# Decay masks of a linear-attention start written by blocks of the triangle, without filling products, with its steps reordered

## The chip, the cores and the metric

The kernel runs on one core of a Trainium2 chip. The metric is the device time of one execution in microseconds (us); the kernel before takes 508.67 us (median of three runs, 508.61 to 508.83). The engines are named as in the profile: PE is TensorE, PEld its weight loads, DVE is VectorE, ACT is ScalarE, POOL is GpSimd, SP is SyncE. PSUM is the memory that PE writes its products to; it is used here in banks of 128 x 512 float32, 2 in the pool `pacc`, 4 in `pmm` and 2 in `patt`.

## The reference

Three layers follow one another: a chunked linear attention with decays (4 batches, 8 heads, 768 steps, head width 32, state 16), a gated feed-forward layer with an RMS norm (256 to 1536 to 256), and a second feed-forward layer with a time shift (256 to 1024 to 256).

```python
for c in range(nc):
    cum = np.cumsum(la, axis=-1)                       # la: log of the decays a
    L = np.exp(cum[:, :, :, None] - cum[:, :, None, :])
    L = L * causal                                     # 0 where j > i
    M = np.einsum('bhin,bhjn->bhij', Cc, Bc) * L
    y_intra = np.einsum('bhij,bhjd->bhid', M, xc)
    y_inter = np.einsum('bhin,bhnd->bhid', Cc, state) * decay_to_i[:, :, :, None]
    ...
xn = x / rms * rms_g
x = (silu(xn @ w_gate) * (xn @ w_val)) @ w_out
...
k = np.maximum(xk @ w_k, 0.0); v = k * k @ w_v
out = sigmoid(xr @ w_r) * v
```

## The kernel before

The kernel works in chunks of 128 steps, six in all (t = 0 to 5), with all four batches side by side: a tile has 128 partitions and 512 columns. While PE multiplies chunk t through the first feed-forward layer (`ffn1`, twelve units u of 128 hidden columns; `g` and `v` are the two products of a unit, `hf` their gated product, `h` its split into two float32r parts, `x` the sum over units), the other engines prepare the attention of the next chunk. Every product with a weight is made of three float32r products (lines 748, 749, 750: high by high, low by high, high by low). The weights arrive as float64, and DVE and ACT convert them while the first chunk runs (`wst`, `wt`, and at last `wgh` and `wgl`, `wvh` and `wvl`, `woh` and `wol`; lines 268, 275, 273, 279, 288, 289).

Before the first product of `ffn1` the attention of chunk 0 has to be done in full, and that of chunk 1 is begun. Their decays L are made on PE and ACT: a bank `Eb` holds, for 4 heads, the matrix (j on partitions, i on columns) of cum(i) - cum(j). First it gets a mask, 0 where i >= j and -30000 elsewhere: a bf16 product of the unit matrix `eye` with `before`, repeated for 4 heads (`spread_eye`, line 380). Then a product with 32 rows adds the sums (`spread_e`, line 393; two batches lie on different rows of the array and their products start together), and ACT takes the exponential (`exp_e`, tile `E`). Chunks 0 and 1 take 8 banks each, all from the four of `pmm`.

The string `START` is the order in which the steps of this beginning are written down: `q` is `spread_eye` ahead of time, `e` and `x` the decays of chunks 0 and 1, `s` and `S` the score products `sc`, `m` and `M` the masking on DVE, `y` the products with x, `n` the RMS norm, `c`, `P` and `z` weight conversions, `k` constants. `fill` puts in extra float32 products (line 637) that nobody reads; `FILL` says where, once in each half of the norm `n`. The written order is not the order of the program: `arrange` runs a list scheduler (`Order`) over all instructions with prices of its own (and with those of `costs`), and fixes the order on each engine. In it an earlier written step wins where two are ready. So a change at the start moves instructions much later as well.

In `ffn1` the tiles g and v take their banks from `pmm` in turn, so that v of unit 3 gets its bank when `hf` of unit 1 (DVE, line 792) has read v of unit 1. The attention of chunk 1 puts its products `y<-Ch,Sf` (line 569), `y<-E,x` (line 527) and `y<-x,Bd` (line 533) between those of the first units.

Of the kernel before, what the change touches and what calls it, by code (L numbers as in the profile page):

```python
# [9 lines left out]
F32 = mybir.dt.float32  # L10
# [6 lines left out]
P = 128  # L17
# [4 lines left out]
T = NB * P  # L22
# [14 lines left out]
        (99, 99, 99, 99, 99, 99, 99, 99, 99, 99, 99, 99, 99))  # L37

HIGH_ACT = ((0, 1, 2, 3, 4, 5, 6, 7, 10, 11), (2, 7))
START = 's0 k0 q0 q1 l0 p0 e0 l1 p1 m0 m1 e2 s1 m2 m3 y0 y1 y2 n0 c0 c1 P0 y3 x0 x2 d0 L0 u0 L1 n1 P1 z0 t0 S0 M1 k1 M0'  # L40
SPARE, LATE_E, BEHIND = ((0, 0), (0, 1), (1, 0)), (), (('n0', 'n1'),)
LOW_POOL, ON_POOL = (), ()

SUB_DVE, MIX_UNIT = tuple(range(27)), 9
MEANS, SPREAD, LOAD_E = (6, 10), 11, (3, 6)
WARM, COLD, HALVED, FILL = (9,), 11, 2, {('n', 0): 1, ('n', 2): 1}

TABLES = {AF.Ln: "natural_log_exp_and_others", AF.Exp: "natural_log_exp_and_others",
          AF.Silu: "silu_and_others", AF.Sigmoid: "sigmoid_and_others"}
# [28 lines left out]
def tile_kernel(ctx: ExitStack, tc, a_c, x_t, B_t, B_s, C_s, B_p, C_p, C_h, kc,  # L78
                w_gate, w_val, w_out, w_k, w_v, w_r, out):
    nc = tc.nc  # L80
    slots, chains, groups, gates, urgent, ranks, costs = {}, [], [], [], [], {}, {}
# [15 lines left out]
    pacc = Pool("pacc", 2, bass.MemoryType.PSUM)  # L97
    pmm = Pool("pmm", 4, bass.MemoryType.PSUM)
# [50 lines left out]
    eye = wp.tile([P, P], BF16, name="eye")  # L149
    before = wp.tile([P, P], BF16, name="before")  # L150
# [154 lines left out]
    A = {c: {} for c in range(NC + 2)}  # L305
# [68 lines left out]
            placed(left, spread_l[c], ML, 2)  # L374

    def spread_eye(c, b):
        for half in range(2):
            pool, tag = (pacc, "acc") if c and b in LATE_E else (pmm, "mm")
            ps = A[c]["Eb", b, half] = pool.tile([P, T], F32, tag=tag, name="Eb")
            mm = nc.tensor.matmul(ps, eye, before.unsqueeze(1).broadcast_to([P, 4, P]), start=True, stop=False)  # L380
            if len(costs) < COLD:
                costs[mm.ins.name] = 427.0
            A[c]["eye", b, half] = mm.ins.name

    def spread_e(c, pair):
        for b in pair:
            if ("Eb", b, 0) not in A[c]:
                spread_eye(c, b)
        for half in range(2):
            for b in pair:  # L390
                g = slice(32 * b, 32 * b + 32)
                eyes = [A[c]["eye", k, half] for k in pair]
                mm = nc.tensor.matmul(A[c]["Eb", b, half], spread_l[c][g, half], spread_r[c][g].rearrange("p h i -> p (h i)"),
                                      start=False, stop=True)
                chains.extend((one, mm.ins.name) for one in eyes)
                if b % 2:
                    costs[mm.ins.name] = 90.0
# [354 lines left out]
    def ffn1(t, hook):  # L752
        xn = [A[t]["xn", k] for k in range(2)]
        acc, hs = [], {}

        def contract(u):
            h = hs.pop(u)
            if u == 0:
                acc.extend(pacc.tile([P, T], F32, tag="acc", name=f"x2_{m}") for m in range(2))
            for m in range(2):  # L760
                mm3(acc[m], wo, u, m, h, u == 0, u == NU - 1)

        gv = {}

        def up(u, parts=(slice(0, T),)):
            for s in parts:
                for n, w in (("g", wg), ("v", wv)):
                    if (n, u) not in gv:
                        gv[n, u] = pmm.tile([P, T], F32, tag="mm", name=n)
                    for k in range(2):  # L770
                        mm3(gv[n, u], w, k, u, xn[k], k == 0, k == 1, s)

        for u in range(NU):
            hook("ab", u)
            if t == 0 and u < HALVED:
                if u == 0:
                    for s in cols:
                        for w in range(HALVED):
                            up(w, (s,))
            else:  # L780
                up(u)
            g, v = gv.pop(("g", u)), gv.pop(("v", u))
            if t <= 1:
                sl = t2("sl")
            elif u % 2 == 0:
                sls = t4("sl")
                sl = sls[:, 0, :]
            else:
                sl = sls[:, 1, :]
            hf = t2("hf")  # L790
            tabled(out=sl, in_=g, func=AF.Silu)
            nc.vector.tensor_mul(hf, sl, v)  # L792
            hs[u] = pair("hl", "h")
            split(hs[u], hf, act_e,
                  pool_e if t == 1 and u in LOW_POOL else vec_e)
            if u >= 2:
                contract(u - 2)

        def tail():
            for u in (NU - 2, NU - 1):  # L800
                contract(u)

        return acc, tail
# [89 lines left out]
    def warm_up(n, pool, tag):  # L893
        w = pool.tile([P, T], F32, tag=tag, name="warm")
        for k in range(n):
            mm = nc.tensor.matmul(w, ones, ones.unsqueeze(1).broadcast_to([P, 4, P]), start=True, stop=True)
            if len(costs) < COLD:
                costs[mm.ins.name] = 427.0 if costs else 900.0
# [26 lines left out]
    def exps(c, b):  # L925
        spread_e(c, (b, b + 1))
        for k in (b, b + 1):
            for half in range(2):
                exp_e(c, k, half)
# [29 lines left out]
    def late_decayed(_):  # L959
        for b in range(NB):  # L960
            decayed_b(0, b)

    stage = dict(e=lambda b: exps(0, b), s=lambda two: scores(0, two), S=lambda two: scores(1, two), M=lambda b: masked(1, b), L=lambda part: load_x(1, part), z=more, t=lambda _: table(AF.Silu), m=masks, y=squares, n=norms, c=convert0, P=lambda u: first[3](u),
                 l=sums, p=placed_e, x=lambda b: exps(1, b), d=late_decayed, u=lambda _: states0(),
                 k=lambda n: (norm_eye, scan_masks)[n](), w=lambda n: warm_up(n, patt, "at"), q=lambda b: spread_eye(0, b))
    for step in START.split():
        at = len(list(nc.cur_bb.bb.instructions))
# [27 lines left out]
    for t in range(NC):  # L995
        c, e = t + 1, t + 2
# [105 lines left out]
        x2, tail = ffn1(t, hook)  # L1102
        if t == 0:
# [9 lines left out]
            x2 = [x2s[:, m] for m in range(2)]  # L1113
# [298 lines left out]
```

## Time and profile before

| | before |
|---|---|
| median of three runs | 508.67 us (508.61 to 508.83) |
| profiled execution | 508.6 us, of it the span 506.6 us |
| PE busy | 500.2 us, 99% of the span |
| DVE busy | 375.7 us, 74% |
| ACT busy | 307.9 us, 61% |
| first product of `ffn1` starts | 24.88 us |
| granted TensorE clock in the records | 1.00 |

The span runs from the first to the last instruction; the profiled execution has 2.0 us around it. A timeline row gives a start, the length of the group, the engine, the line, the operation, the tiles and the number of instructions; plain float32 products (`sc`, `y`, `ss`, the filling ones) have two records each. A product's record lasts longer than the distance to the next one, because products overlap; the distance between two starts is what it costs.

### The profile page before, as it was taken

What the parts mean: (1) busy time and instruction counts of PE and PEld (TensorE: products, weight loads), DVE (VectorE), ACT (ScalarE), POOL (GpSimd) and SP (SyncE); (2) the same over time, 40 slices, a digit from 0 to 9 for tenths busy, and PEclk for the clock granted to TensorE, in tenths of its full rate; (3) what the DMA queues carried; (4) which work ended last, traced back from release to release, by engine and by line L of the source; (5) the groups of instructions that cost most, each with busy time, mean ns of one, the idle gap of its engine ahead of it and who ended that gap; (6) DMA issues with size and microseconds to landing.
All of it is one profiled execution on the core that took longest, in us unless ns stands there. A gap on an engine that the chain in (4) does not pass through costs nothing.

```text
span 506.6 us, 7497 instructions
## 1 busy us (share of the span) xinstructions
PE 500.2 (99%) x2869; PEld 406.8 (80%) x2869; DVE 375.7 (74%) x610; ACT 307.9 (61%) x509; POOL 10.4 (2%) x26
## 2 busy tenths in 40 slices
PE   8999999999999999999999999999999999999997
PEld 4687887788888888888888888888888888888885
DVE  6899998988698965479995659996628763335672
ACT  5999798566589744457763456764358643345552
POOL 1100000000010000010000010000000000000000
PEclk9999999999999999999999999999999999999999
DMA  8868755342321220152111141110000000000101
GB/s 257 230 204 276 261 175 193 105 137 93 123 85 43 78 82 13 57 174 77 42 58 68 46 162 44 65 48 36 0 1 1 18 25 1 1 1 0 42 0 42
DMA packets 23283, 42.60 MB, mean 84 GB/s; under 512 B 3136, under 2 KB 6720, under 8 KB 23248
## 3 DMA queue, kind: packets, MB, share of 16 engines
q1 hardware_dynamic: 20496, 33.41, 20.0%
q10 hardware_dynamic: 2752, 8.72, 5.1%
q8 instruction: 22, 0.36, 0.3%
q14 instruction: 13, 0.11, 0.1%
HBM read 38.52 MB, written 3.34 MB: 83 GB/s over the span
## 4 chain that ended last, share of the span: by engine, by line
PE 91%; DVE 5%; ACT 2%; issue 1%; DMA 1%; DVEq 0%; ACTq 0%
PE v L748 10%; PE v L750 10%; PE v L749 10%; PE g L748 6%; PE x L748 6%; PE x L749 6%; PE x L750 6%; PE g L749 6%; PE g L750 6%; PE kp L748 4%; PE kp L750 4%; PE kp L749 4%; PE y L527 2%; PE sc L442 1%; PE rps L750 1%; PE rps L749 1%
## 5 line engine op out<-in xcount | busy, mean ns | idle before, releaser
L792 DVE TENSOR_TENSOR hf<-sl,v 128x512 f32<-128x512 f32 x72 | 49.0, 683 | 50.0 <-PE v L750 49.5
L140 ACT CAST h<-hf 128x512 fp32r<-128x512 f32 x72 | 44.4, 617 | 60.8 <-DVE hf L792 60.7
L133 ACT ACTIVATE sl<-g 128x512 f32<-128x512 f32 x72 | 42.8, 595 | 44.9 <-PE g L750 44.6
L143 DVE TENSOR_TENSOR h<-hf,h 128x512 fp32r<-128x512 f32 x72 | 50.5, 701 | 24.1 <-ACT h L140 24.1
L748 PE MATMUL g<-xn,wgh 128*128 128x512 f32 (+1 forms) x148 | 58.0, 392 | 0.4 <-DVE E L514 0.4
L749 PE MATMUL g<-xn,wgl 128*128 128x512 f32 (+1 forms) x148 | 57.0, 385 | 0.4 <-DVE wgl L289 0.4
L748 PE MATMUL v<-xn,wvh 128*128 128x512 f32 (+1 forms) x148 | 57.0, 385 | 0.0
L750 PE MATMUL g<-xn,wgh 128*128 128x512 f32 (+1 forms) x148 | 56.8, 384 | 0.0
L749 PE MATMUL v<-xn,wvl 128*128 128x512 f32 (+1 forms) x148 | 56.8, 384 | 0.0
L750 PE MATMUL v<-xn,wvh 128*128 128x512 f32 (+1 forms) x148 | 56.8, 383 | 0.0
L749 PE MATMUL x<-h,wol 128*128 128x512 f32 x144 | 56.3, 391 | 0.0
L748 PE MATMUL x<-h,woh 128*128 128x512 f32 x144 | 55.8, 391 | 0.1
L750 PE MATMUL x<-h,woh 128*128 128x512 f32 x144 | 55.2, 389 | 0.0
L867 DVE TENSOR_TENSOR k<-rl 128x512 f32<-128x512 f32 x40 | 30.0, 749 | 15.0 <-ACT rl L863 15.0
L143 DVE TENSOR_TENSOR h<-k,h 128x512 fp32r<-128x512 f32 x48 | 32.8, 686 | 10.3 <-ACT h L140 9.9
L140 ACT CAST h<-k 128x512 fp32r<-128x512 f32 x48 | 29.7, 619 | 16.5 <-DVE k L867 16.3
L748 PE MATMUL kp<-xm,wkh 128*128 128x512 f32 x96 | 37.7, 393 | 0.0
L750 PE MATMUL kp<-xm,wkh 128*128 128x512 f32 x96 | 37.4, 390 | 0.0
L749 PE MATMUL kp<-xm,wkl 128*128 128x512 f32 x96 | 37.4, 389 | 0.0
L748 PE MATMUL v<-h,wvvh 128*128 128x512 f32 x96 | 37.3, 389 | 0.0
L749 PE MATMUL v<-h,wvvl 128*128 128x512 f32 x96 | 37.3, 389 | 0.0
L863 ACT ACTIVATE rl<-kp 128x512 f32<-128x512 f32 x48 | 28.5, 594 | 14.1 <-PE kp L750 13.4
(157 smaller groups left out, 983.0 us busy)
## 6 DMA issues: line engine op xcount, KB each, us to landing
E<-la_r ACTq DMA_DIRECT2D x16, 512.0 KB
x<-in_x_t SPq DMA_DIRECT2D x6, 512.0 KB
wst<-in_w_gate SPq DMA_DIRECT2D x6, 512.0 KB
wst<-in_w_val SPq DMA_DIRECT2D x6, 512.0 KB
wst<-in_w_out SPq DMA_DIRECT2D x6, 512.0 KB
Br<-in_B_s SPq DMA_DIRECT2D x12, 256.0 KB
Cr<-in_C_s SPq DMA_DIRECT2D x12, 256.0 KB
out<-r SPq DMA_DIRECT2D x11, 256.0 KB
```

Source lines behind the costliest of these rows:

```text
L133: one = nc.scalar.activation(out=out, in_=in_, func=func, **kw).ins.name
L140: last[1] = nc.scalar.copy(x[:, 0, :], src).ins
L143: last[0] = le.tensor_tensor(out=x[:, 1, :], in0=src, in1=f32(x[:, 0, :]), op=ALU.subtract).ins
L442: nc.tensor.matmul(bank[:, q * 256:(q + 1) * 256], bs[:, p, :], cs[:, p, :, :].rearrange("p a i -> p (a i)"), start=True, stop=True)
L527: nc.tensor.matmul(y[half][32 * j:32 * j + 32, at[half]:at[half] + P], x[:, b, h * D:(h + 1) * D], m[:, h, :], start=start and at[half] == ...
L748: nc.tensor.matmul(ps[:, s], w[0][:, k, ws], x[:, 0, s], start=first, stop=False, skip_group_check=s.stop - s.start < T)
L749: nc.tensor.matmul(ps[:, s], w[1][:, k, ws], x[:, 0, s], start=False, stop=False, skip_group_check=s.stop - s.start < T)
L750: nc.tensor.matmul(ps[:, s], w[0][:, k, ws], x[:, 1, s], start=False, stop=last, skip_group_check=s.stop - s.start < T)
L792: nc.vector.tensor_mul(hf, sl, v)
L863: marks.append(nc.scalar.activation(out=rl, in_=kp, func=AF.Relu).ins.name)
L867: nc.vector.tensor_mul(k2, rl, rl)
```

## The change

The mask of a bank is no longer one product of 128 rows and 512 columns. Columns i < 64 of each head get a product of 128 rows and 256 columns (4 heads of 64). Columns i >= 64 are never masked for j < 64, so only the block j >= 64, i >= 64 is written, by a product of 64 rows and 64 partitions with 256 columns; the banks of the two halves use different rows of the array for it, rows 0 to 63 and rows 64 to 127, so that two of them can run at once. The filling products are left out. In `START`, `k0` and `q0` stand ahead of `s0`, and `x2`, the second half of the decays of chunk 1, stands behind `n1`, `P1` and `z0`. `LATE_E`, which was empty, goes.

```diff
-START = 's0 k0 q0 q1 l0 p0 e0 l1 p1 m0 m1 e2 s1 m2 m3 y0 y1 y2 n0 c0 c1 P0 y3 x0 x2 d0 L0 u0 L1 n1 P1 z0 t0 S0 M1 k1 M0'
-SPARE, LATE_E, BEHIND = ((0, 0), (0, 1), (1, 0)), (), (('n0', 'n1'),)
+START = 'k0 q0 s0 q1 l0 p0 e0 l1 p1 m0 m1 e2 s1 m2 m3 y0 y1 y2 n0 c0 c1 P0 y3 x0 d0 L0 u0 L1 n1 P1 z0 x2 t0 S0 M1 k1 M0'
+SPARE, BEHIND = ((0, 0), (0, 1), (1, 0)), (('n0', 'n1'),)
...
-WARM, COLD, HALVED, FILL = (9,), 11, 2, {('n', 0): 1, ('n', 2): 1}
+WARM, COLD, HALVED, FILL = (9,), 11, 2, {}
...
     def spread_eye(c, b):
+        views = []
         for half in range(2):
-            pool, tag = (pacc, "acc") if c and b in LATE_E else (pmm, "mm")
-            ps = A[c]["Eb", b, half] = pool.tile([P, T], F32, tag=tag, name="Eb")
-            mm = nc.tensor.matmul(ps, eye, before.unsqueeze(1).broadcast_to([P, 4, P]), start=True, stop=False)
+            ps = A[c]["Eb", b, half] = pmm.tile([P, T], F32, tag="mm", name="Eb")
+            views.append(ps.rearrange("p (h i) -> p h i", h=4))
+            mm = nc.tensor.matmul(views[half][:, :, :P // 2], eye, before[:, :P // 2].unsqueeze(1).broadcast_to([P, 4, P // 2]),
+                                  start=True, stop=False, skip_group_check=True)
             if len(costs) < COLD:
-                costs[mm.ins.name] = 427.0
+                costs[mm.ins.name] = 214.0
+        for half in range(2):
+            g = slice(half * P // 2, (half + 1) * P // 2)
+            mm = nc.tensor.matmul(views[half][P // 2:, :, P // 2:], eye[g, g], before[g, g].unsqueeze(1).broadcast_to([P // 2, 4, P // 2]),
+                                  start=False, stop=False, skip_group_check=True)
+            costs[mm.ins.name] = 20.0 if half else 120.0
             A[c]["eye", b, half] = mm.ins.name
```

What the scheduler makes of it is seen in three places. Lines from 380 on have a number higher by 1 to 7 in the changed kernel. First, PE at the very start, up to the first products that add the sums (line 393, now 400); before:

```order
L380 LDWEIGHTS eye
L380 MATMUL Eb<-before,eye 128x512
L476 MATMUL sc<-Cr,Br 128x256 x8
L380 LDWEIGHTS eye
L380 MATMUL Eb<-before,eye 128x512
L380 LDWEIGHTS eye
L380 MATMUL Eb<-before,eye 128x512
L380 LDWEIGHTS eye
L380 MATMUL Eb<-before,eye 128x512
L393 MATMUL Eb<-wvvh,wkh 128x512 x4
```

and in the changed kernel:

```order
L381 LDWEIGHTS eye
L381 MATMUL Eb<-before,eye 128x4x64
L381 LDWEIGHTS eye
L381 MATMUL Eb<-before,eye 128x4x64
L387 LDWEIGHTS eye
L387 MATMUL Eb<-before,eye 64x4x64
L387 LDWEIGHTS eye
L387 MATMUL Eb<-before,eye 64x4x64
L483 MATMUL sc<-Cr,Br 128x256 x8
```

Two whole banks are masked ahead of the scores instead of one, and two behind them instead of three. Where a bank comes free alone (the next four of chunk 0, and half of those of chunk 1) one product of 128 rows and one of 64 rows stand alone, one behind the other. Second, DVE from the masking of chunk 1 to the gated products `hf` of units 0 and 1; `wgl` and `wvl` are the low parts of the weights of units 2 and 3. Before:

```order
L514 TENSOR_TENSOR E<-sc,E 128x512
L492 SCALAR_TENSOR_TENSOR decay<-decay,lmask 128x516
L289 TENSOR_TENSOR wgl<-wt_146,wgh 128x2x256
L289 TENSOR_TENSOR wvl<-wt_146,wvh 128x2x256
L792 TENSOR_TENSOR hf<-sl,v 128x512
L268 TENSOR_SCALAR wst_314<-wst_314 128x1024
L792 TENSOR_TENSOR hf<-sl,v 128x512
L143 TENSOR_TENSOR h<-hf,h 128x512
```

and in the changed kernel:

```order
L521 TENSOR_TENSOR E<-sc,E 128x512 x2
L627 TENSOR_TENSOR Sf<-state,k_sb 128x512
L289 TENSOR_TENSOR wgl<-wt_146,wgh 128x2x256
L289 TENSOR_TENSOR wvl<-wt_146,wvh 128x2x256
L799 TENSOR_TENSOR hf<-sl,v 128x512
L268 TENSOR_SCALAR wst_321<-wst_321 128x1024
L499 SCALAR_TENSOR_TENSOR decay<-decay,lmask 128x516
L143 TENSOR_TENSOR h<-hf,h 128x512
L279 SCALAR_TENSOR_TENSOR wt_545<-wt_545,wst_321 128x1024
L799 TENSOR_TENSOR hf<-sl,v 128x512
```

The scan of the decays went from ahead of `wgl` to behind the first `hf`, and the second `hf` now stands behind the scan, an `h` and a conversion. `Sf` stood earlier, between the `xn` of the norm. Third, PE where the attention of chunk 1 puts its first `y` between the products of units 0 to 4; before, from the last product of v of unit 3:

```order
L750 MATMUL v<-xn,wvh 128x512
L569 MATMUL y<-Ch,Sf 128x128 x2
L748 MATMUL x_0_591<-h,woh 128x512
L748 MATMUL x_1_592<-h,woh 128x512
L569 MATMUL y<-Ch,Sf 128x128 x2
L749 MATMUL x_0_591<-h,wol 128x512
```

and, nine weight products further on,

```order
L750 MATMUL x_1_592<-h,woh 128x512
L527 MATMUL y<-E,x 32x128 x5
L748 MATMUL g<-xn,wgh 128x512
L527 MATMUL y<-E,x 32x128 x2
L748 MATMUL v<-xn,wvh 128x512
```

and in the changed kernel, from the last product of x of unit 1:

```order
L757 MATMUL x_1_606<-h,woh 128x512
L576 MATMUL y<-Ch,Sf 128x128 x4
L534 MATMUL y<-E,x 32x128 x7
L755 MATMUL g<-xn,wgh 128x512
L534 MATMUL y<-E,x 32x128
L540 MATMUL y<-x,Bd 32x64
L755 MATMUL v<-xn,wvh 128x512
```

The same work goes through in two visits of `y` instead of four, all behind the twelve products of x for units 0 and 1. Further on the order is nearly the same on every engine; the sums of squares of chunk 1's second half (`ss`, line 685) stand one weight product earlier.

## Rows read from the trace of the kernel before

**Rows 1.** The page: busy time with its share of the span; the chain by engine.

```profile
PE 500.2 (99%) x2869; PEld 406.8 (80%) x2869; DVE 375.7 (74%) x610; ACT 307.9 (61%) x509; POOL 10.4 (2%) x26
...
PE 91%; DVE 5%; ACT 2%; issue 1%; DMA 1%; DVEq 0%; ACTq 0%
```

**Rows 2.** Windows: length, busy PE, PEld, DVE, ACT, POOL, clock, DMA share, GB/s.

```profile
5.00:12.00 7.00, 6.33 (x52) 2.85 (x51) 6.41 (x16) 4.86 (x11) 0.00 (x0) 1.00 1.00 332
...
20.00:31.00 11.00, 10.76 (x84) 8.42 (x82) 10.38 (x22) 10.77 (x19) 0.00 (x0) 1.00 0.76 231
31.00:42.00 11.00, 10.63 (x57) 7.54 (x58) 11.00 (x20) 9.60 (x15) 0.00 (x0) 1.00 0.63 215
```

**Rows 3.** Timeline of PE, 31 to 43 us: units 2 and 3, then `y`.

```profile
31.50 0.50 PE L749 MATMUL g<-xn,wgl 128*128 128x512 f32 x1 [0.37 <-DVE wgl L289]
...
35.51 0.39 PE L748 MATMUL v<-xn,wvh 128*128 128x512 f32 x1
...
36.64 0.39 PE L750 MATMUL v<-xn,wvh 128*128 128x512 f32 x1
36.96 0.49 PE L569 MATMUL y<-Ch,Sf 64*128 64x128 f32 x4
37.38 0.73 PE L748 MATMUL x<-h,woh 128*128 128x512 f32 x2
...
42.62 0.40 PE L749 MATMUL g<-xn,wgl 128*128 128x512 f32 x1
```

**Rows 4.** Timelines of DVE and PE, two later waits.

```profile
79.66 1.22 DVE L279 SCALAR_TENSOR_TENSOR wt<-wt,wst 128x1024 int32<-128x1024 int32 x1 [1.14 <-ACT wt L273]
...
100.97 0.50 PE L748 MATMUL g<-xn,wgh 128*128 128x512 f32 x1 [0.36 <-DVE E L514]
```

**Rows 5.** Timeline of PE, 18 to 25 us: norm, decays of chunk 1.

```profile
18.78 0.60 PE L637 MATMUL ss<-ones 128*128 128x256 f32 x2
19.21 0.38 PE L380 MATMUL Eb<-before,eye 128*128 128x512 bf16 x1
...
21.49 0.61 PE L380 MATMUL Eb<-before,eye 128*128 128x512 bf16 x2
21.93 0.39 PE L720 MATMUL ss<-tiny 128*128 128x128 f32 x2
...
24.88 0.39 PE L748 MATMUL g<-xn,wgh 128*128 128x256 f32 x1
```

**Rows 6.** Timeline of PE, 6 to 12 us: decays of chunk 0.

```profile
6.95 0.82 PE L380 MATMUL Eb<-before,eye 128*128 128x512 bf16 x3
7.71 0.73 PE L393 MATMUL Eb<-wvvh,wkh 32*128 32x512 f32 x4
...
10.17 0.50 PE L393 MATMUL Eb<-wvvh,wkh 32*128 32x512 f32 x2
10.60 0.39 PE L380 MATMUL Eb<-before,eye 128*128 128x512 bf16 x1
10.92 0.50 PE L393 MATMUL Eb<-wvvh,wkh 32*128 32x512 f32 x2
11.35 0.65 PE L527 MATMUL y<-M,x 128*32 128x128 f32 x16
```

**Rows 7.** Line 476, the scores: what its idle time waited for (us, times).

```profile
  DMA Br<-in_B_p: 0.2, 1
```

**Rows 8.** Timeline of ACT around the first exponentials of chunk 1.

```profile
19.58 0.40 ACT L288 CAST wvh<-wt 128x256 fp32r<-128x256 f32 x1
20.11 1.08 ACT L133 ACTIVATE E<-Eb 128x512 f32<-128x512 f32 x2
```

**Rows 9.** Timeline of DVE, 29 to 36 us.

```profile
29.64 1.22 DVE L492 TENSOR_TENSOR_SCAN decay<-decay,lmask 128x516 f32<-128x516 f32 x1
30.78 0.67 DVE L289 TENSOR_TENSOR wgl<-wt,wgh 128x512 fp32r<-128x512 f32 x1
...
34.97 1.22 DVE L279 SCALAR_TENSOR_TENSOR wt<-wt,wst 128x1024 int32<-128x1024 int32 x1
```

More of the change, by code (lines that the diff above doesn't have):

```diff
@@ L393, in spread_e @@
                 mm = nc.tensor.matmul(A[c]["Eb", b, half], spread_l[c][g, half], spread_r[c][g].rearrange("p h i -> p (h i)"),
-                                      start=False, stop=True)
+                                      start=False, stop=True, skip_group_check=True)
                 chains.extend((one, mm.ins.name) for one in eyes)
```

## Prediction

> **What bounds the kernel now.** I read the page first: PE is busy for 99% of the span, and of the chain that ended last 91% is PE, 5% DVE and 2% ACT [rows 1]. So a change pays only where PE does work that may be left out, or waits. The windows show where that is: PE lacks 0.67 us of 7 from 5 to 12, 0.24 of 11 from 20 to 31 and 0.37 of 11 from 31 to 42 us, and in the last two DVE and ACT are nearly full as well (10.38 and 10.77, then 11.00 and 9.60) [rows 2]: up to 42 us three engines take turns at being late. The timeline names the two waits behind the first product of `ffn1` that the trace charges to another engine: at 31.50 us PE waits for `wgl`, at 100.97 for DVE's masking [rows 3, 4]. Otherwise the weight products follow one another at 0.227 us (from 35.51 to 36.64 five take 1.13 [rows 3]). A shift reached at 42 us is a shift of the end, unless a later wait eats it.
>
> **The masks.** Two old masks amid products of full size take 0.44 us, 0.22 each (21.49 to 21.93) [rows 5]. One that is followed by 32-row products takes 0.32 (10.60 to 10.92) [rows 6]: a change of tile shape costs 0.10 us. A pair of new masks takes twice 0.11, one change, and 0.11 for both blocks together: 0.43 us, as much as two old ones. That the blocks overlap is an estimate from the 32-row products, of which two leave PE after 0.43 us with both changes and the weight load (10.17 to 10.60) [rows 6]; without overlap it is 0.11 more. A mask that stands alone takes 0.11 + 0.10 + 0.11 = 0.32 us in place of 0.22: 0.10 us **lost**. The trace has no 64-by-64 product. The bounds for a lone mask are 0.22 us (the change costs nothing) and 0.45 (the change brings a weight load of 0.1, as the pair at 10.17 does); I take 0.32, since a full-size mask behind 32-row products shows no such load (0.32 from 10.60).
>
> [...]
>
> *The start.* The scores ahead of 6.95 us wait 0.2 us for a transfer of their B [rows 7], so the second mask that now stands ahead of them, 0.2 us long, is hidden by it (else it costs 0.2). Behind them two masks are left: 0.43 us and a change, some 0.55 in place of 0.76 (6.95 to 7.71) [rows 6], and the products that add the sums start 0.2 us sooner. The next four banks come free one after another from ACT, and there the masks stand alone: two lie on the path to 10.92, 0.10 us each. What is left at 11.35, where the products with x begin, is 0.0 us (bounds: 0.2 sooner, 0.25 later).
>
> *The filling products.* Each takes 0.43 us of PE (18.78 to 19.21) [rows 5]. The first holds up the masks and sums of chunk 1, and with them ACT: its `wvh` ends at 19.98, of which the last 0.06 us would lie under a next instruction, and the exponentials start at 20.11 [rows 8], 0.19 us behind where they could follow. Without it ACT goes on at once. The second pair of exponentials hangs on a bank that the first frees and on a lone mask, so some 0.17 us remains (bounds 0 and 0.19). The second filling product pays for the lone masks of chunk 1 and their changes, and PE reaches the first product of `ffn1` at 24.88 as before [rows 5] (0.2 either way; the wait of the next item covers that).
>
> *`wgl` and the gated products.* In the new order DVE has the same work ahead of `wgl`, without the scan: 30.78 less 1.14 (29.64 to 30.78) [rows 9], less 0.17 (ACT's lead), and less some 0.15 of the 0.6 us that DVE idles from 20 to 31 us [rows 2], as `xn` waits less: 29.3 us. The wait at 31.50 goes; 0.37 us in its row [rows 3], about 0.5 with the weight load. But the second `hf` now stands behind more work, and v of unit 3 needs its bank. From 29.3: `wgl`, `wvl`, `hf`, the clip, `h` and `hf` at 0.60 each (the 0.67 of the row of `wgl`, the last 0.08 under the next), scan and conversion at 1.14 each [rows 9]: 3.6 + 2.3 = 5.9, 35.25 us with the signal. PE, unhindered, would be at v of unit 3 half a microsecond before 35.51, and waits there up to 0.4 us: it starts at 35.25, **-0.26 us** (bounds: -0.5 if DVE is in time, 0 if DVE gains nothing).
>
> *Visits of `y`.* From 35.51 to 42.62 PE takes 7.11 us [rows 3]: 20 weight products (4.54), five passes of `y` of 0.22 (1.10; a visit with one pass takes 0.42, 36.96 to 37.38, with a change and the first weight load), and so 1.47 for four visits, 0.37 each. Two visits instead of four save 0.74; the passage from 64-row to 32-column `y` inside the first costs 0.12: **-0.62 us**. The x products now come ahead of `y` and need `wol`. DVE has it done 1.8 us behind the second `hf` (clip, Ch, `wol`, 0.60 each), at 37.06, and PE comes for it at 35.25 + 8 x 0.227 = 37.07. Were DVE 0.3 us later, this term would shrink by as much.
>
> *Later.* At 42.6 us PE is 0.88 us ahead, DVE by less, with idle time further on to make it up. The sums of squares of chunk 1 come one weight product (0.23 us) sooner still. The norm and ACT's conversion follow them, and DVE's at 79.66, which waits 1.14 us for ACT [rows 4]; if DVE is full from there to the wait at 100.97, that stretch moves by the whole lead and up to 0.23 more: **-0.2 us** (bounds 0 and -0.23).
>
> Sum: -0.26 - 0.62 - 0.2 = -1.1 us. The profiled execution took 508.6 us, so 507.5; the median of the runs stands 0.07 above it: 507.6 us.
>
> **The rivals.**
> 1. *The lead is lost to DVE and ACT.* They are full between 20 and 42 us [rows 2], and their order is fixed. If a new wait of 0.4 us arises there (`hf` of unit 1 or `wol` late by that), and DVE's smaller lead is what counts up to 79.66, the sum is -0.26 + 0.4 - 0.62 and nothing later: -0.5 us, 508.1. For it: DVE's 11.00 of 11. Against it: the 1.14 us at 79.66 show that DVE has room before it sets the next stretch [rows 4].
> 2. *The masks cost more.* If a change around the 64-row block costs 0.2 us, or the blocks do not overlap, each lone mask or pair adds 0.1. Two lone ones lie ahead of 11.35, and ACT and DVE follow from there; with the lone one of chunk 1: +0.3, 507.9 us. For it: a 32-row pair keeps PE for 0.43 us, twice its 0.22.
> [...]
> 4. *The change does nothing:* what it removes was covered, and the visits take as long in their new order: 508.7.
>
> **How the numbers follow.** About 0.2% (1.0 us) is what a measurement of this kernel can tell from no change, and my sum ends just on its far side. Forecast (0.7 to 1.5 us gained) 0.55, rival 1 0.24, rival 2 0.10, rival 3 0.05, rival 4 0.06. Of the forecast's chance 0.38 lies beyond 1.0 us and 0.17 short of it; 0.08 of rivals 1 and 2 lies beyond it too, if they go the other way (DVE in time for the bank, changes cheaper than 0.10). Faster 0.46; same 0.17 + 0.26 + 0.04 = 0.47, where 0.04 is most of rival 4; slower 0.07, rival 3 and the rest of rival 4. The range reaches up past rival 1 to 508.5, and down to where no wait for the bank arises (-0.3) and the masks are cheap (-0.4 in all their places): 506.9.
>
> **What would show it.** Right: the first sums' products at about 7.5 us and the products with x at 11.3 to 11.4; exponentials of chunk 1 at 19.9; first product of `ffn1` at 24.7 to 25.1; no wait for `wgl`; a wait of 0.3 to 0.5 us ahead of v of unit 3, which starts at 35.2 to 35.3; two visits of `y`, and g of unit 4 going on at 41.7; clock 1.00. Wrong: a lone mask of over 0.45 us; `wgl` later than 30.5; a wait for `wol`; a lead at 102 us that is not larger than that at 42 by 0.2.

## The result and the profile after

The changed kernel takes 511.41 us (median of 20 executions, 508.85 to 516.18), the kernel before 508.77 in the same series: a ratio of 1.0065, 95% interval 1.0041 to 1.0089. It is slower by 0.65%, where 507.6 us was forecast. A ratio leaves out executions over 1.5% above the fastest of their kernel; the counts of the experiments have them all. The profiled execution took 510.03 us, of it the span 507.9.

The page names no new limit. PE's share of the busy time and of the chain is nearly that of [rows 1]:

```profile
PE 501.7 (99%) x2881; PEld 408.6 (80%) x2881; DVE 375.6 (74%) x610; ACT 307.8 (61%) x509; POOL 10.4 (2%) x26
...
PE 90%; DVE 4%; DMA 3%; SPq 1%; ACT 1%; issue 1%; DVEq 0%; ACTq 0%
```

The windows from 18 to 32 us show what is new (columns as in [rows 2], the clock behind the count of POOL):

```profile
18.00:20.00 2.00, 1.61 (x12) 1.04 (x11) 1.95 (x9) 1.63 (x7) 0.00 (x0) 1.00 0.76 225
20.00:22.00 2.00, 1.75 (x9) 1.00 (x10) 1.48 (x4) 2.00 (x6) 0.00 (x0) 1.00 0.45 111
22.00:24.00 2.00, 2.00 (x10) 0.68 (x8) 1.88 (x6) 2.00 (x5) 0.00 (x0) 0.54 0.95 332
24.00:26.00 2.00, 2.00 (x16) 1.38 (x18) 1.34 (x4) 2.00 (x4) 0.00 (x0) 0.50 0.84 217
26.00:28.00 2.00, 2.00 (x14) 1.27 (x11) 0.81 (x2) 1.98 (x4) 0.00 (x0) 0.50 1.00 378
28.00:30.00 2.00, 2.00 (x15) 2.00 (x15) 2.00 (x3) 1.11 (x2) 0.00 (x0) 0.75 0.45 113
30.00:32.00 2.00, 2.00 (x19) 2.00 (x19) 2.00 (x5) 2.00 (x4) 0.00 (x0) 1.00 0.38 100
```

From about 22 to 29 us the granted clock is 0.50; in [rows 2] it is 1.00. Ahead of the fall PE is idle for 0.39 us of two and 0.25 of the next two. The timeline of PE shows where, in answer to [rows 5]:

```profile
18.32 0.50 PE L660 MATMUL ss<-ones,sq 128*128 128x1 f32 x4
...
19.11 0.50 PE L400 MATMUL Eb<-wvvh,wkh 32*128 32x512 f32 x2
20.04 0.49 PE L727 MATMUL ss<-tiny 128*128 128x128 f32 x2 [0.43 <-DVE tiny L719]
20.74 0.27 PE L381 MATMUL Eb<-before,eye 128*128 128x256 bf16 x1 [0.21 <-ACT E L133]
...
24.66 2.49 PE L483 MATMUL sc<-Cr,Br 32*128 32x256 f32 x16
27.08 0.58 PE L755 MATMUL g<-xn,wgh 128*128 128x256 f32 x1
```

PE waits 0.43 us for DVE's `tiny`, a step of the norm, and 0.21 us for a bank that ACT frees. Then the clock falls, the sixteen scores take 2.4 us, and the first product of `ffn1` starts at 27.08, 2.20 us later than in [rows 5]. The end is 1.39 us later than before (the last weight product starts at 503.97 us instead of 502.58): from 27 us on the change gains.

The other rows that answer to those of before, PE's timelines for [rows 6] and [rows 3]:

```profile
6.72 0.39 PE L381 MATMUL Eb<-before,eye 128*128 128x256 bf16 x2
7.04 0.30 PE L387 MATMUL Eb<-before,eye 64*64 64x256 bf16 x2
7.27 0.73 PE L400 MATMUL Eb<-wvvh,wkh 32*128 32x512 f32 x4
...
9.42 0.27 PE L381 MATMUL Eb<-before,eye 128*128 128x256 bf16 x1
9.62 0.29 PE L387 MATMUL Eb<-before,eye 64*64 64x256 bf16 x1
9.85 0.50 PE L400 MATMUL Eb<-wvvh,wkh 32*128 32x512 f32 x2
...
11.14 0.65 PE L534 MATMUL y<-M,x 128*32 128x128 f32 x16
```

```profile
34.01 0.40 PE L756 MATMUL g<-xn,wgl 128*128 128x512 f32 x1
...
37.88 0.39 PE L755 MATMUL v<-xn,wvh 128*128 128x512 f32 x1
...
44.37 0.39 PE L756 MATMUL g<-xn,wgl 128*128 128x512 f32 x1
```

The wait for `wgl` is gone (34.01, no bracket), and from v of unit 3 to g of unit 4 it is 6.49 us instead of the 7.11 of [rows 3].

### The profile page after: what moved, and what is told of

Read it like the earlier page. It is cut to its first block, busy times and chain, and to the rows that moved or that the text cites. A ratio compares the mean times of both kernels' runs of the same rounds, so it can differ in the third digit from the quotient of the medians.

```text
span 507.9 us, 7520 instructions
## 1 busy us (share of the span) xinstructions
PE 501.7 (99%) x2881; PEld 408.6 (80%) x2881; DVE 375.6 (74%) x610; ACT 307.8 (61%) x509; POOL 10.4 (2%) x26
## 4 chain that ended last, share of the span: by engine, by line
PE 90%; DVE 4%; DMA 3%; SPq 1%; ACT 1%; issue 1%; DVEq 0%; ACTq 0%
PE v L755 10%; PE v L756 10%; PE v L757 10%; PE g L755 6%; PE g L756 6%; PE g L757 6%; PE x L755 6%; PE x L756 6%; PE x L757 6%; PE kp L755 4%; PE kp L757 4%; PE kp L756 4%; PE y L534 2%; DMA Bt<-in_B_t 1%; DMA Br<-in_B_p 1%; PE sc L449 1%
```

## The experiments

Two readings stood against each other. One: order and masks are worth what was forecast, and the clock costs more. The other (rival A below): order and masks lose time by themselves, and the clock is a companion. Among those that blame the clock it was open what lets it fall: the missing filling products, the smaller masks (theories B and M), or PE's waits (theory I).

The granted clock differs from execution to execution of one kernel (a mean of 0.976 to 0.999 in 20 of the changed one), so each series is told by counts: executions with a mean granted clock of 0.995 or more, of 0.988 to 0.994, and below 0.988; all are counted, since the clock is the question. "At 1.00" is the median of those whose mean is 1.000. A mean of 0.995 or more is not a full clock throughout. In e2's profile (509.67 us at a mean of 0.997) it is 0.50 from 16.13 to 19.54 us. The profiles of e4, e7, e12 and e14 are slow there too: the 32 products `u<-x,Bd` take 1.08 us in each and 0.65 in e13's, and e14's window from 18 to 20 us has 0.50. Two windows of e2:

```profile
12.00:18.00 6.00, 5.98 (x90) 3.72 (x91) 4.63 (x10) 5.92 (x18) 1.53 (x4) 0.84 1.10 311
18.00:20.00 2.00, 2.00 (x40) 1.83 (x31) 1.24 (x4) 0.59 (x3) 0.00 (x0) 0.61 0.63 212
```

The runs e1 to e3 and e5 shared one chip, and so did e0, e4, e6 and e7, e8 to e11, and e12 to e14; the kernel before ran beside each of these series.

| kernel | 0.995 up | 0.988 to 0.994 | below | at 1.00, us | median, us |
|---|---|---|---|---|---|
| before (four series) | 120 | 4 | 9 | 508.51 | 508.6 to 508.8 |
| changed (two series) | 4 | 17 | 10 | none | 511.41, 510.51 |
| e1 changed, filling put back | 5 | 2 | 5 | 509.57 | 511.30 |
| e2, e10 before, no filling | 24 | 0 | 0 | 508.35, 508.31 | 508.55, 508.46 |
| e3 before, masks by blocks | 7 | 0 | 5 | 509.09 | 509.57 |
| e4 changed, whole masks | 6 | 6 | 0 | 507.60 | 508.83 |
| e5 changed, products in the waits, bank of the norm | 0 | 8 | 4 | none | 512.57 |
| e6 changed, products in the waits, own bank | 7 | 2 | 3 | 507.92 | 509.44 |
| e7, e8 as e6, whole masks | 22 | 0 | 2 | 507.61, 507.40 | 507.64, 507.94 |
| e9 as e6, blocks of 128 rows twice | 11 | 1 | 0 | 509.89 | 509.83 |
| e11, e13 as e6, wait at 8 us filled too | 24 | 0 | 0 | 507.76, 507.57 | 507.81, 507.67 |
| e12 as e13, whole masks | 11 | 1 | 0 | 507.50 | 508.00 |
| e14 changed, only the wait at 8 us filled | 0 | 9 | 3 | none | 511.35 |

Wherever a kernel gets products added, they are kept out of the scheduler and put behind a named instruction (`extras`), so that the order of all others is untouched on every engine. In e3 the blocks of 64 rows are put in that way. In e4 the order of the changed kernel is written into the kernel as numbers, less the blocks of 64 rows.

**e1, the filling put back in the new order.**

```diff
-WARM, COLD, HALVED, FILL = (9,), 11, 2, {}
+WARM, COLD, HALVED, FILL = (9,), 11, 2, {('n', 0): 1, ('n', 2): 1}
...
-            costs[mm.ins.name] = 430.0
-            chains.extend((one, mm.ins.name) for one in behind)
+            extras.append((behind[0], mm.ins.name))
```

> The changed kernel, in its own order on every engine, with the two filling products put back behind the broadcasts of the norm of chunk 0 (as before the change). They are no part of the output. Theory (without the filling products the clock falls; order and masks are as good as forecast): granted clock 1.00 in every window, first product of ffn1 at 24.7 to 25.2 us, no late start left, 507.2 to 508.0 us. Rival A (new order and masks lose the time by themselves, the clock only goes with it): 508.7 us or more at clock 1.00. Rival B (the smaller masks, not the filling products, let the clock fall): the clock falls between 18 and 30 us as in the changed kernel, 510 to 516 us.

Ratio 1.0049 (1.0014 to 1.0083): still slower, and the theory as stated fails. At a clock of 1.00 the median is 509.57 us, which is in the range of rival A, but neither order nor masks need to be behind it. The last weight product of e1's profile starts 1.89 us behind that of e13 (below: the same order and masks, its waits filled). Of this 1.08 us lie ahead of the second masks (7.64 against 6.56), where PE's first products still run slowly (last section), and the two filling products take 0.44 us each. The profile, of an execution that kept its clock, shows that the filling does not fill the waits (PE, then DVE):

```profile
19.22 0.60 PE L644 MATMUL ss<-ones 128*128 128x256 f32 x2
19.66 0.50 PE L659 MATMUL ss<-ones,sq 128*128 128x1 f32 x4
...
21.37 0.49 PE L726 MATMUL ss<-tiny 128*128 128x128 f32 x2 [0.43 <-DVE tiny L718]
22.07 0.27 PE L381 MATMUL Eb<-before,eye 128*128 128x256 bf16 x1 [0.21 <-ACT E L133]
```

```profile
20.49 0.16 DVE L712 TENSOR_SCALAR tiny<-ss 128x2 f32<-128x2 f32 x1 [0.44 <-ACT tiny L133]
```

In the new order the sums of squares `ss` stand behind the filling product, and the norm on ACT and DVE hangs on them: it comes as much later as PE is kept busy, and both waits stay.

**e2 and e10, the filling taken out of the old order.**

```diff
-            mm = nc.tensor.matmul(ps, f32(ones), f32(ones).unsqueeze(1).broadcast_to([P, 2, P]), start=True, stop=True, skip_group_check=True)
+            mm = nc.tensor.matmul(ps[:, :2], f32(ones), f32(ones)[:, :2], start=True, stop=True, skip_group_check=True)
```

Two of the 256 columns stay, and the price in the scheduler, so that the order is the old one.

> The kernel before in its own order, with the two filling products cut from 256 columns to 2, so that only their work is gone (they are no part of the output). Theory: the granted clock falls to 0.5 for some microseconds between 18 and 30 us, 510 to 514 us. Rival A and rival B: the clock stays at 1.00, and the time is that of before less at most 0.4 us, 508.3 to 508.8 us.

> The kernel before without its filling products (cut to 2 columns) once more, for its waits at full clock and for more executions. If the old order keeps the clock without filling: at least 9 of 12 runs at 0.995 or more, 507.9 to 509.8 us. If the 12 runs were luck: 4 or more below 0.995. PE's wait ahead of the norm's second broadcast is then 0.5 to 0.7 us (0.19 in the kernel before, and the 0.43 of the filling product).

Ratios 0.9985 (0.9964 to 1.0007) and 0.9988 (0.9970 to 1.0005), and 24 of 24 executions have a mean clock of 0.995 or more: in the old order the filling is not needed. Nor is the wait what e10 expected; PE's timeline in e10:

```profile
18.51 0.28 PE L637 MATMUL ss<-ones 128*128 128x2 f32 x2
...
19.67 0.49 PE L720 MATMUL ss<-tiny 128*128 128x128 f32 x2 [0.21 <-DVE tiny L712]
20.27 0.38 PE L380 MATMUL Eb<-before,eye 128*128 128x512 bf16 x1
```

It stays at 0.21 us, and no second one follows that the trace charges to an engine: 0.21 against the 0.64 of the changed kernel. The missing filling is not the cause; the longer waits of the new order and the smaller masks are left.

**e3, the masks alone in the old order.**

```diff
-            mm = nc.tensor.matmul(ps, eye, before.unsqueeze(1).broadcast_to([P, 4, P]), start=True, stop=False)
+            mm = nc.tensor.matmul(v[:, :, :P // 2], eye, before[:, :P // 2].unsqueeze(1).broadcast_to([P, 4, P // 2]),
+                                  start=True, stop=False, skip_group_check=True)
...
+            low = nc.tensor.matmul(v[P // 2:, :, P // 2:], eye[g, g], before[g, g].unsqueeze(1).broadcast_to([P // 2, 4, P // 2]),
+                                   start=False, stop=False, skip_group_check=True)
+            extras.append((mm.ins.name, low.ins.name))
```

> The kernel before in its own order, filling products kept, with the masks by blocks alone: each 128x128 mask becomes one product of 128 rows on half of the columns and one of 64 rows, the latter behind the last mask of a run of masks. Theory: granted clock 1.00; a lone mask with its change takes 0.43 us, two banks 0.55 up to the 32-row products (both as in the changed kernel's trace), so nothing is gained: 508.5 to 509.1 us. Rival A (the masks lose time): 509.2 us or more at clock 1.00. Rival B: the clock falls between 18 and 30 us, 510 us or more.

Ratio 0.9995 (0.9968 to 1.0022). At a clock of 1.00 it is 509.09 us, 0.6 above before: the blocks gain nothing. Five of 12 executions fall below 0.988 (516.8 to 519.2 us), where the kernel before has 5 of 35 in the same series. The profile is of one of the five. PE waits 0.45, 0.22 and 0.22 us for banks from 8 to 9.5 us, and the clock is 0.50 from 10.7 to 34.6 us, from far ahead of the norm:

```profile
5.00:12.00 7.00, 6.11 (x47) 2.97 (x50) 6.45 (x15) 4.81 (x11) 0.00 (x0) 0.91 0.99 342
12.00:18.00 6.00, 6.00 (x70) 4.31 (x63) 3.09 (x6) 3.58 (x10) 1.52 (x4) 0.50 1.08 317
34.00:36.00 2.00, 2.00 (x19) 1.50 (x13) 1.09 (x3) 2.00 (x5) 0.00 (x0) 0.85 0.03 9
```

So there is an early fall beside the one at 22 us, and the masks by blocks seem to bring it more often, in the old order and with the filling in place; 12 executions do not prove it. Rival B had the fall at 18 to 30 us.

**e4, whole masks in the new order.**

```diff
+    order = np.cumsum(np.frombuffer(zlib.decompress(base64.b85decode(PLAN)), np.int16).astype(int)).tolist()
```

> The changed kernel's order on every engine, without filling products, but with whole 128x128 masks: each stands where its block of 128 rows stands in the changed kernel, and the blocks of 64 rows are gone. What is left of the change is the reordering and the missing filling. Theory M (the smaller masks leave PE less to do between its waits from 5 to 24 us, and that lets the clock fall in most executions): at least 9 of 12 runs at a mean clock of 0.995 or more, and their times 507.0 to 508.2 us, since lone masks take 0.2 us less as well. Rival O (the order without filling lets it fall): most runs below 0.995, median 510 us or more. Rival A (the order loses time by itself): 508.8 us or more at a clock of 1.00.

Ratio 0.9999 (0.9981 to 1.0017). Neither theory holds alone. At full clock it takes 507.60 us, so the new order loses no time: for the order, rival A is out. Half of the executions still fall to 0.989 to 0.992, with whole masks, and none below 0.988. PE's timeline has the waits of the new order. Its products are slow from about 17 to 20 us (the 32 of `u<-x,Bd` take 1.08 us, 0.65 in e13) and again from 23.8 (three masks take 1.47, 0.90 in e7):

```profile
22.00 0.49 PE L719 MATMUL ss<-tiny 128*128 128x128 f32 x2 [0.55 <-DVE tiny L711]
22.70 0.38 PE L379 MATMUL Eb<-before,eye 128*128 128x512 bf16 x1 [0.21 <-ACT E L133]
```

**e5 and e6, products in the two waits.** In e5 they go to the bank of the norm; the second stands behind the other half of the broadcast, not where its expectation puts it. In e6 they go to a bank of `pacc` that nobody reads, and stand in the two waits.

```diff
+                w = pacc.tile([P, T], F32, tag="acc", name="gap")
+                gaps.extend(nc.tensor.matmul(w[:, :n * P], f32(ones), f32(ones).unsqueeze(1).broadcast_to([P, n, P]), start=True, stop=True,
+                                             skip_group_check=True).ins.name for n in (2, 1))
...
+                    extras.append((mm.ins.name, gaps[0]))
```

> The changed kernel, in its own order, with two filling products at the two places where its PE waits between 18 and 22 us: one of 256 columns (0.43 us) behind the first sums of chunk 1 (0.43 us of waiting ahead of the norm's second broadcast), one of 128 columns (0.21 us) behind that broadcast (0.21 us of waiting). No part of the output. Theory (the clock falls because PE idles there): clock 1.00 in every window, and the filling costs nothing: 507.0 to 507.8 us, some 0.2 less than with the filling products at their old places. If the filling helps only where it stood, behind 21.6 us too: the clock falls, 509 to 514 us.

> The changed kernel in its own order, with products of 256 and 128 columns in its two waits between 19.5 and 20.8 us, written to a bank that nobody reads (in the run before, DVE waited 0.96 us for such a product, as it wrote to the bank of the norm). No part of the output. Theory I (PE's waits from 18 to 22 us decide): at least 9 of 12 runs at a mean clock of 0.995 or more, 507.5 to 508.8 us. Theory M: the waits near 8 us and the short masks stay, so at least 4 of 12 runs fall below 0.995. Rival O: as theory I.

e5: ratio 1.0081 (1.0045 to 1.0118), no execution reaches 0.995, against its theory. DVE, which PE waits for, now waits for the product itself, and PE's wait doubles to 0.84 us; DVE's timeline:

```profile
20.50 0.48 DVE L745 SCALAR_TENSOR_TENSOR xnf<-yT,k_sb,ss 128x256 f32<-128x256 f32 x1 [0.96 <-PE ss L737]
```

e6: ratio 1.0025 (0.9995 to 1.0055); 7 of 12 are at 0.995 or more, against 4 of 31 without; theory I wanted 9, and theory M's four falls or more are there, three of them below 0.988. Its fastest execution takes 507.56 us. The waits between 19.5 and 20.8 us look like one cause (e13 and e14 compare them side by side); 5 of 12 still fall.

**e7 and e8, the same with whole masks.** The edits of e4 and e6 together.

> The kernel with the changed order and whole masks, and the same two products in PE's waits on a bank of their own. Theories M and I: at least 10 of 12 runs at a mean clock of 0.995 or more, 507.0 to 508.2 us, faster than before. Rival A: 508.8 us or more at a clock of 1.00.

> The kernel with the changed order, whole masks and the two products in PE's waits once more, on whichever chip comes. If it is the better version: at least 9 of 12 runs at a mean clock of 0.995 or more, those at 507.3 to 508.1 us, and faster than before. If the runs at full clock were luck: half of them fall, median above 508.5 us.

Ratios 0.9976 (0.9959 to 0.9993) and 0.9974 (0.9952 to 0.9996): faster than the kernel before by a quarter of a per cent, twice, and so faster than the changed kernel. Two executions of e7 fall to 0.975 (516.2 us).

**e0, the control.** The changed kernel again, beside e4, e6 and e7.

> The changed kernel once more, as the control beside the other three. Theory M, I and O alike: most runs below a mean clock of 0.995, median 510 to 514 us; the runs of the highest clock at 507.6 to 509.1 us (rival A: none under 508.7).

Ratio 1.0041 (1.0026 to 1.0056), median 510.51 us, its fastest 509.08 at 0.996. The last bracket of the expectation is not answered: no execution was near 1.00.

**e9, the blocks of 128 rows twice.**

```diff
+            more = nc.tensor.matmul(views[half][:, :, :P // 2], eye, before[:, :P // 2].unsqueeze(1).broadcast_to([P, 4, P // 2]),
+                                    start=True, stop=False, skip_group_check=True)
+            extras.append((mm.ins.name, more.ins.name))
```

> The changed kernel with the two products in PE's waits, and each 128-row block of a mask computed twice (the second overwrites the first), so that PE passes as many columns for a mask as with whole ones, but still changes the tile shape. Theory M (too little work of the short masks): at most 2 of 12 runs at a mean clock under 0.988; at full clock 507.8 to 508.8 us, as each mask on the path costs 0.1 us. Rival T (the change of tile shape, or the 64-row products, lets the clock fall): 3 or more of 12 under 0.988.

Ratio 1.0010 (0.9991 to 1.0030), none below 0.988: as theory M expects; the three or more of rival T did not come. The time at full clock was underrated by a microsecond. The last weight product of its profile starts 2.51 us behind that of e13; 1.22 of it lie ahead of the second masks (7.78 against 6.56), where PE's first products still run slowly, as in e1.

**e11 to e14, the wait near 8 us.** Two products with zero weights go into PE's wait of 0.45 us ahead of the third run of masks. In e11 they changed the scores in two banks of chunk 0, so that its output is not the reference's; from e12 on each bank's sums are started once, and the scores stay.

```diff
+                        one = nc.tensor.matmul(A[0]["sc", 0, k], zero, before.unsqueeze(1).broadcast_to([P, 4, P]), start=False, stop=True,
+                                               skip_group_check=True)
+                        extras.append((mm.ins.name, one.ins.name))
...
-                                      start=True, stop=True)
+                                      start=k == 0, stop=True, skip_group_check=True)
```

> The changed kernel with the two products in its waits between 19.5 and 20.8 us, and two products more, of 512 columns with zero weights, in PE's wait of 0.45 us near 8 us; they add 0.0 to banks of scores that are read later. Theory W (the wait near 8 us together with the short masks behind it lets the clock fall early): at most 1 of 12 runs at a mean clock under 0.988, 507.4 to 508.5 us at full clock. Rival T (the masks' form, whatever PE does in the wait): 3 or more of 12 under 0.988.

> Changed order, whole masks, the two products in the waits between 19.5 and 20.8 us, and two products of zero weights in the wait near 8 us. They add 0.0 to banks of scores, whose sums are now started once per bank, so that the output stays the reference's. Theory W: no run below a mean clock of 0.995, 507.2 to 508.2 us at full clock, median 507.5 to 508.2, faster than before. If that wait has no part in it: 1 to 3 of 12 runs below 0.995, as in the two series without these products.

> The changed kernel (masks by blocks) with the same four products, scores kept. Theory W: at most 1 of 12 runs below 0.995, 507.5 to 508.3 us at full clock. Rival T (the masks' form by itself): 3 or more below 0.988.

> The changed kernel with the two products of zero weights near 8 us alone; its waits between 19.5 and 20.8 us stay open. If the two places work independently (theories W and I): no run below 0.988, but at least 6 of 12 between 0.988 and 0.994, at 509.8 to 512.8 us, which come from the fall at 22 us. If the wait near 8 us decides for both: 10 or more of 12 at 0.995 or more. If only chance made the early falls rarer: 3 or more below 0.988.

e11: 0.9975 (0.9957 to 0.9993). e13: 0.9985 (0.9970 to 1.0001), the changed kernel itself with its three waits filled: all 12 executions at 0.997 or more. At 1.00 it takes 507.57 us with the new order and the masks by blocks, so rival A is out for both together. e14: 1.0055 (1.0035 to 1.0075), none at 0.995, so the wait at 8 us does not decide for the later fall. Three of 12 are at 0.983, the number that its expectation gave for mere chance in the early falls; theory W had none. Its windows show waits and the later fall in turn:

```profile
22.00:24.00 2.00, 1.69 (x8) 0.95 (x9) 1.53 (x5) 2.00 (x6) 0.00 (x0) 0.93 0.91 269
24.00:26.00 2.00, 2.00 (x10) 0.86 (x9) 1.56 (x5) 1.89 (x5) 0.00 (x0) 0.50 0.99 348
```

e12: 0.9991 (0.9975 to 1.0008); one execution at 0.990, which is not its theory but the other case of its expectation (1 to 3), and no gain over e7 that could be seen.

## Why the prediction was wrong

At a full clock the forecast's sum came out, and the clock did not stay full. The step that failed is the item on the filling products: it has ACT go on at once, and PE with it. In its place PE waits twice, 0.43 us at 20.04 and 0.21 at 20.74, and behind these waits the clock is 0.50 from 22.2 to 29.0 us, which costs 2.5 us in the profiled execution. A clock that falls was the case of rival 3, which was given 0.05. How far it would fall, and behind what, no row of before shows: the 1.00 of [rows 2], with PE idle for 0.67 us of 7 from 5 to 12 us, is one execution of one kernel; of 133 executions of the kernel before, 13 fall below 0.995 as well.

e13, the changed kernel with its three waits filled, shows the change at full clock, and its profile can be set against the forecast term by term. PE's timeline and windows:

```profile
19.38 0.70 PE L739 MATMUL gap<-ones 128*128 128x256 f32 x2
19.92 0.45 PE L743 MATMUL ss<-tiny 128*128 128x128 f32 x2
20.20 0.39 PE L739 MATMUL gap<-ones 128*128 128x128 f32 x2
20.58 0.27 PE L384 MATMUL Eb<-before,eye 128*128 128x256 bf16 x1
...
24.89 0.39 PE L773 MATMUL g<-xn,wgh 128*128 128x256 f32 x1
...
35.29 0.50 PE L773 MATMUL v<-xn,wvh 128*128 128x512 f32 x1 [0.21 <-DVE hf L817]
...
41.94 0.39 PE L774 MATMUL g<-xn,wgl 128*128 128x512 f32 x1
```

```profile
20.00:31.00 11.00, 11.00 (x88) 8.79 (x88) 10.35 (x22) 10.97 (x20) 0.00 (x0) 1.00 0.85 270
31.00:42.00 11.00, 10.79 (x65) 7.86 (x65) 11.00 (x19) 9.40 (x16) 0.00 (x0) 1.00 0.53 182
```

- **Masks and start.** A pair of masks takes 0.55 us up to the 32-row products in the changed kernel (6.72 to 7.27), as forecast; a lone one 0.43 (9.42 to 9.85), with both changes. The first product of `ffn1` starts at 24.89 in e13, forecast 24.88. At 11.35, where the forecast has 0.0 (at most 0.2 sooner), e13 is at 10.99, 0.36 sooner, and at `ffn1` nothing of it is left. e8, with whole masks, is 0.27 us ahead of e13 at the first of these places (10.72) and 0.38 at the second (24.51). The blocks are at best no gain: 0.35 us lost by the last weight products of these two profiles (501.14 against 501.49), nothing to 0.2 by the medians at full clock (507.57 in e13 against 507.61 and 507.40 in e7 and e8).
- **The filling products.** The term of -0.17 failed: the exponentials of chunk 1 start at 20.10 in the changed kernel, as in [rows 8]. I had ACT go on at once, but the changed order puts the sums of squares behind both halves of the broadcast, and ACT waits for them:

```profile
18.86 0.26 ACT L133 ACTIVATE tiny<-ss,k_sb 128x2 f32<-128x2 f32 x1 [0.31 <-PE ss L660]
...
20.10 1.07 ACT L133 ACTIVATE E<-Eb 128x512 f32<-128x512 f32 x2
```

  DVE's `tiny` hangs on this step of ACT, and PE's 0.43 us at 20.04 on `tiny`. I had no wait there. (That ACT's conversions lie under the next instruction by 0.06 us was my estimate; in the trace of before it is 0.10, 19.29 + 0.39 against 19.58.) e1 shows the same chain, and e6, e7 and e13 fill the waits at its end.
- **`wgl`, the bank of v of unit 3, `y`.** Forecast 35.25 with a wait of up to 0.4; e13 has 35.29 with 0.21, which is -0.22 for -0.26. From there to g of unit 4 e13 takes 6.65 us, 0.46 less than in [rows 3], as the first product, behind the wait, takes 0.11 us more up to the next one; the changed kernel, which does not wait there, takes 6.49, which is the 0.62 less that was forecast. At g of unit 4 e13 leads by 0.68 us (41.94 against 42.62), where 0.88 was forecast.
- **Later.** The lead of e13 is 0.87 us at 51.44 (50.57 in e13), as a later visit of `y` takes 0.20 us less, of which the forecast has nothing. It is 1.10 us at 82.64 (81.54), as forecast (-0.2), and 1.09 at the end.
- **Sum.** -1.09 us in e13's profile, -0.94 by the medians at 1.00 (507.57 against 508.51); forecast -1.1. That it fits so well is in part luck: the 0.20 us of the later visit make up for what the item before lacked. PE's start differs from execution to execution (the second masks start at 6.56 us in e13 and at 6.72 in the changed kernel; last section), so one profile is no finer than that.
- **Rival 3**, slower by the clock, came true, but not for want of filling: the old order does without it (e2, e10: 24 of 24 executions at 0.995 or more). The profiled execution takes 510.03 us, with the low clock from 22.2 to 29.0. The median is 1.4 us higher still, as ten of the 20 executions take 512.4 us or more.

So the measured slowdown is what the clock takes, less the gain of 1.1 us. The clock takes 2.5 us in the profiled execution (1.39 later at the end, where e13 is 1.09 earlier), up to 8.6 in others (516.18 against 507.57).

That the waits between 19.5 and 20.8 us let it fall in the new order is shown: e13 and e14, side by side, differ only in the two products that fill these waits, and 12 of 12 executions against 0 of 12 are at 0.995 or more.

For the executions below 0.988 less is shown. They come with masks by blocks: 10 of 31 in the changed kernel, 3 to 5 of 12 in e1, e3, e5, e6 and e14; with whole masks none of 12 in e4 and e12, none of 24 in e2 and e10, 2 of 24 in e7 and e8, and 9 of 133 in the kernel before. None came in the 24 of e11 and e13, where the wait near 8 us is filled too, and none in the 12 of e9, where it is open and the masks have more columns. But e14's three came with that wait filled, and e6 ran on another chip than e11 and e13. Whether the wait or the short masks decide is open, and only e3 has a profile of such an execution.

Open is also how much is needed for the fall at 22 us: e1's profile has the same two waits and no fall (1.00 in every window from 5 to 36 us). And with all waits filled the clock is not always full: 7 of the 36 executions of e11 to e13 have a mean of 0.997 and take 509.3 to 510.1 us; e12's profile is one of them, with slow products from about 17 to 20 us (the 32 of `u<-x,Bd` take 1.08). No run looks for the cause of that fall. It was not tried to fill e1's waits, or to move the sums of squares back between the two halves of the broadcast.

## What to carry to other kernels

In this kernel's start, where PE works in small pieces, two waits of 0.43 and 0.21 us cost 2.5 us in the profiled execution, as the clock was 0.50 behind them for 6.8 us. So price a shorter PE step also by the wait that it opens, and look at several executions' granted clock before calling it safe. A product that only keeps PE busy belongs into the wait itself, on a bank that nobody waits for: in e1 and e5 it held up the very engine that PE waited for (0.44 us a product in e1, 0.96 us of DVE's waiting in e5), in e7 it cost nothing that can be seen (507.61 us at a clock of 1.00, and 507.60 without it in e4). An order is to be judged at equal clock, by the shift of one and the same product along the program, and with the same start of PE.

## What the runs showed of the hardware

One and the same kernel is granted different clocks: 20 executions of the changed one lie at 508.9 to 509.1, 509.9 to 510.4, 512.4 to 512.8, about 514.0 and 515.9 to 516.2 us, with mean granted clocks of 0.996 to 0.999, 0.992 to 0.993, 0.985 to 0.989, 0.983 and 0.976. PE's first products also differ in speed: the first two blocks of 128 rows take 0.65 us in e1's profile and 0.39 in e13's, in PE's timelines (and e2 and e10, one and the same kernel, have 0.65 and 0.39 for their first mask). The granted clock does not tell it: the windows from 1 to 8 us in e1's have 1.00, and both executions a mean of 1.000. What makes the difference is not shown.

```profile
5.06 0.65 PE L381 MATMUL Eb<-before,eye 128*128 128x256 bf16 x2
```

```profile
4.93 0.39 PE L384 MATMUL Eb<-before,eye 128*128 128x256 bf16 x2
5.26 0.30 PE L390 MATMUL Eb<-before,eye 64*64 64x256 bf16 x2
```

The two 64-row products on different halves of the array do run together: 0.23 us for both, with a change of shape (7.04 to 7.27 in the changed kernel), as long as one of them takes alone (9.62 to 9.85).
